# A polysketch attention and SwiGLU kernel on one core: the first batch cut into blocks of 384, 320 and 384 tokens, half of the third block's units multiplied by parts, and the key sums regrouped

## The chip, the cores and the metric

The kernel runs on one core of a Trainium2 chip. The engines of that core work side by side, each in its own order: TensorE (PE, matrix products into PSUM; PEld is its weight load), VectorE (DVE), ScalarE (ACT), GpSimd (POOL) and SyncE (SP), whose queue issues most of the DMA transfers. They wait for each other with semaphores. The metric is the device time of one execution in microseconds; lower is better. Three executions of the kernel before took 278.57, 278.71 and 279.0 us, so the median is 278.71.

## The reference

Inputs are q, k and v of 4 batches, 4 heads, 1088 tokens and 32 values (float32), two sketches S1 and S2 of 8 x 32, and the weights w_gate and w_val (128 x 1536) and w_out (1536 x 128). The sketches and weights come in 64-bit floats.

```python
def phi(x):                                   # 32 values -> 64 features
    a = np.einsum('rd,bhsd->bhsr', S1, x)
    b = np.einsum('rd,bhsd->bhsr', S2, x)
    return np.einsum('bhsi,bhsj->bhsij', a, b).reshape(*x.shape[:-1], r * r)
q_p, k_p = (phi(q), phi(k))
kv = np.einsum('bhsf,bhsd->bhfd', k_p, v)     # key values
z = np.sum(k_p, axis=2)                       # key sums
num = np.einsum('bhsf,bhfd->bhsd', q_p, kv)
den = np.einsum('bhsf,bhf->bhs', q_p, z)[..., None] + 1e-06
x = (num / den) as (4352 tokens, 4 heads * 32 = 128)
g, val = x @ w_gate, x @ w_val
out = (g * (1 / (1 + np.exp(-g))) * val) @ w_out
```

The attention has no softmax: a batch's keys are folded into one 64 x 32 matrix and one vector of 64 sums per head, and the queries are multiplied with these. Behind it stands a SwiGLU layer over all 4352 tokens with 1536 hidden values, by far the larger part of the work.

## The kernel before

**The layer.** Hidden values are cut into 12 chunks of 128. A *unit* (i, j) is chunk j of token block i: it multiplies the block's x with chunk j of w_gate and of w_val, applies SiLU on ScalarE and the product on VectorE, and leaves a tile of hidden values. A *down product* multiplies that tile with chunk j of w_out and adds it up over the 12 chunks in one PSUM bank; when a block's twelve are done, VectorE transposes the sum (`store`) and SP's queue sends it out.

Two kinds of units exist. A plain one (`unit`, matmuls at L1034) multiplies in float32, which the trace shows as two matmul records per product. A unit *by parts* (`start_unit`, L997, and `finish_unit`, L1010 and L1011) replaces each product by three in the single-pass format fp32r: x and the weights are first cut into a high part, a low part and a difference. `start_unit` multiplies the differences, ScalarE scales that PSUM pair in place (L1000), and `finish_unit` adds the two other products; ScalarE's SiLU (L1013) and VectorE's product (L1018) follow. The weights are cut by `cut_weights` (four steps for each quarter of a weight: high part on ScalarE, remainder on VectorE or GpSimd, low part on ScalarE, difference on VectorE or GpSimd, all L871), the tokens by `cut_tokens` (L881, L884, L889).

**The blocks.** The first batch's 1088 tokens are cut into three blocks, of 384, 384 and 320 tokens. Its attention is computed block by block, so that the layer can begin early, and all 36 units of these blocks are plain. The other three batches make seven blocks, six of 480 tokens and one of 384, called the *line*: their 84 units are by parts. In the line, unit y + 1 is started ahead of finishing unit y.

**PSUM.** Eight banks: g0, g1, g2 and acc (banks 0 to 3), and the pairs a (4, 5) and b (6, 7). Plain units take single banks in turn; from unit 17 of the list `seq` on only g0, g1 and g2 are in turn, and acc gathers the first block's down products. `pair` gives a line unit the least recently used of three pairs (g0 with g1, a, b).

**The order.** It is written out by hand; every engine keeps the order in which the program issues its instructions. The attention of batches 1 to 3 is the generator `attentions`, advanced some steps at a time by `parts_of` between units, and by `group` at fixed places in the line. For each batch it turns keys and queries (VectorE transposes, which also issue the next loads on SP's queue), multiplies the key sketches (L354), forms the key features on VectorE (L377, four operations over chunks 0 to 2, 3 to 4, 5 to 6 and 7 to 8, into the tile phk), adds the features of the nine chunks up on GpSimd (`feature_sums`, L547, five additions into zs), multiplies the key values (L388) and the sums (L717), folds them on VectorE (L601 to L608, the result is needed by the query sketches), spreads the key values by six DMAs on SP's queue (`spread_out`), multiplies the query sketches (L342), forms the query features (`query_step`: a denominator, then three rounds of features and transposes), and multiplies the numerators (L780). A place where the generator says `yield` is a place where units come between.

In before, the list `seq` holds 30 plain units behind the six that stand with the first batch's attention. From unit 17 on each is followed by one down product and one step of the second batch's attention, and by steps of the weight cutting. Then come the remaining down products in threes, with the second batch's numerators among them; behind these ("first") the third batch's key features and its five sums, the cutting of the line's first tokens, the first `start_unit`, the last two down products and the line:

```python
        phk = apool.tile([P, NC, H, R, R], FP32, tag="phk", name="phk")
        yield from features(phk, kab)
        zs, sums = feature_sums(phk)
        for f in sums:
            f()
        yield from turn_keys(3)
        yield from turn_queries(2)
        for b in (2, 3):
            yield "pe"
```

In the line, `parts_of` advances the generator by one step after each of the first twenty units, and `group` goes on to the next "pe" ahead of units 4, 6, 20, 22 and 40. What follows the first "pe" is the third batch's key values, key sketches of the fourth, and sums' products.

## Time and profile before

| | us |
|---|---|
| median of three executions | 278.71 |
| the profiled execution | 278.89 |
| its span (first to last instruction) | 277.2 |
| around the span | 1.69 |
| first plain unit's matmul (L1034) | 15.29 |
| first down product (L1082) | 49.01 |
| second batch: key sums on GpSimd (L547) | 63.20 to 68.89 |
| second batch: key values (L388), sums' products (L717), query products (L342) | 67.92, 68.95, 72.31 |
| second batch: numerators (L780) | 86.82 |
| first matmul of the line (L997) | 91.42 |
| third batch: key features (L377) | 91.17 to 93.93 |
| third batch: key sums on GpSimd | 93.49 to 99.34 |
| third batch: key values, sums' products, query products | 98.71, 101.06, 104.93 |

Times within the span are counted from its start. A row of a timeline gives the start, the duration, the engine, the line of the kernel, the operation with what it writes and reads, the shape and how many of them; in brackets stand the idle time of the engine ahead of it and what ended that. Durations overlap a little within an engine, as one operation's tail runs beside the next one's start, so a step is read from start to start. Matmul ends are modelled. In the chain of waits, times are moved by about 0.1 us against the timeline. The granted clock was 1.0 throughout.

### The profile page before, as it was taken

What the parts mean: (1) busy time and instruction counts of PE and PEld (TensorE: products, weight loads), DVE (VectorE), ACT (ScalarE), POOL (GpSimd) and SP (SyncE); (2) the same over time, 40 slices, a digit from 0 to 9 for tenths busy, and PEclk for the clock granted to TensorE, in tenths of its full rate; (3) what the DMA queues carried; (4) which work ended last, traced back from release to release, by engine and by line L of the source; (5) the groups of instructions that cost most, each with busy time, mean ns of one, the idle gap of its engine ahead of it and who ended that gap; (6) DMA issues with size and microseconds to landing.
All of it is one profiled execution on the core that took longest, in us unless ns stands there. A gap on an engine that the chain in (4) does not pass through costs nothing.

```text
span 277.2 us, 5670 instructions
## 1 busy us (share of the span) xinstructions
PE 271.4 (98%) x2169; PEld 198.3 (72%) x2169; DVE 203.7 (74%) x355; ACT 184.5 (67%) x330; POOL 98.9 (36%) x110
## 2 busy tenths in 40 slices
PE   8899999999999999999999999999999999999995
PEld 7645565666766787777577777867887888788994
DVE  3997987977688873887545766967877995987431
ACT  3468665565421586667479898769879878886860
POOL 3313422179820440060034353435425553542000
PEclk9999999999999999999999999999999999999999
DMA  6573195221151123000200020000100200010011
GB/s 192 168 220 79 54 277 185 74 89 57 39 114 28 26 85 94 2 1 0 38 13 4 0 39 0 0 2 10 27 0 2 36 0 1 9 29 0 10 29 28
DMA packets 26139, 14.30 MB, mean 52 GB/s; under 512 B 19840, under 2 KB 24192, under 8 KB 26112
## 3 DMA queue, kind: packets, MB, share of 16 engines
q1 hardware_dynamic: 25456, 13.84, 19.4%
q8 instruction: 17, 0.28, 0.4%
q10 hardware_dynamic: 656, 0.10, 0.2%
q14 instruction: 10, 0.08, 0.1%
HBM read 11.41 MB, written 2.23 MB: 49 GB/s over the span
## 4 chain that ended last, share of the span: by engine, by line
PE 94%; DVE 2%; DMA 2%; ACT 1%; issue 0%; SPq 0%
PE PS L1082 22%; PE PS L1034 16%; PE PS L1010 13%; PE PS L997 13%; PE PS L1011 13%; PE PS L1074 2%; PE PS L1077 2%; PE PS L1076 2%; PE PS L354 2%; PE PS L780 2%; PE PS L342 2%; PE PS L388 2%; DMA kld<-in_k_dram 2%; PE PS L1110 1%; PE PS L497 1%; PE PS L445 1%
## 5 line engine op out<-in xcount | busy, mean ns | idle before, releaser
L1000 ACT ACTIVATE PS<-PS 128x960 f32<-128x960 f32 (+1 forms) x84 | 78.5, 935 | 32.0 <-PE PS L997 31.2
L1018 DVE SCALAR_TENSOR_TENSOR hbuf<-PS,sg 128x480 f32<-128x480 f32 (+1 forms) x84 | 53.7, 640 | 43.6 <-ACT sg L1013 40.8
L1013 ACT ACTIVATE sg<-PS 128x480 f32<-128x480 f32 (+1 forms) x84 | 46.7, 556 | 2.0 <-PE PS L1011 1.2
L997 PE MATMUL PS<-xd,gphq 128*128 128x480 f32 (+1 forms) x84 | 47.3, 564 | 0.0
L1082 PE MATMUL PS<-hbuf,wo 128*128 128x480 f32 (+3 forms) x118 | 45.9, 492 | 0.0
L1010 PE MATMUL PS<-x,graw 128*128 128x480 f32 (+1 forms) x84 | 32.1, 382 | 0.0
L1011 PE MATMUL PS<-x,wb 128*128 128x480 f32 (+1 forms) x84 | 31.6, 376 | 0.0
L997 PE MATMUL PS<-xd,wd 128*128 128x480 f32 (+1 forms) x84 | 31.4, 374 | 0.0
L1010 PE MATMUL PS<-x,w 128*128 128x480 f32 (+1 forms) x84 | 31.4, 374 | 0.0
L1011 PE MATMUL PS<-x,graw 128*128 128x480 f32 (+1 forms) x84 | 31.3, 373 | 0.0
L1034 PE MATMUL PS<-xT,wg 128*128 128x384 f32 (+1 forms) x72 | 28.7, 480 | 0.0
L1034 PE MATMUL PS<-xT,wv 128*128 128x384 f32 (+1 forms) x72 | 28.0, 470 | 0.2 <-DVE wv L286 0.2
L1082 PEld LDWEIGHTS PS<-hbuf,wo 128*128 128x128 f32 x118 | 22.1, 189 | 7.4 <-issue 0.9
L1038 ACT ACTIVATE sg<-PS 128x384 f32<-128x384 f32 (+1 forms) x30 | 13.8, 465 | 18.8 <-PE PS L1034 17.2
L997 PEld LDWEIGHTS PS<-xd,gphq 128*128 128x128 f32 x84 | 15.8, 188 | 10.0 <-ACT PS L1000 6.4
L997 PEld LDWEIGHTS PS<-xd,wd 128*128 128x128 f32 x84 | 15.8, 189 | 9.9 <-issue 6.7
L884 POOL TENSOR_TENSOR x<-xT,x 128x480 fp32r<-128x480 f32 (+1 forms) x6 | 7.2, 1195 | 37.6 <-ACT x L881 37.6
L1034 PEld LDWEIGHTS PS<-xT,wv 128*128 128x128 f32 x72 | 13.4, 190 | 8.9 <-DVE hbuf L1049 0.9
L1034 PEld LDWEIGHTS PS<-xT,wg 128*128 128x128 f32 x72 | 12.9, 189 | 9.3 <-issue 1.2
L1010 PEld LDWEIGHTS PS<-x,graw 128*128 128x128 f32 x84 | 15.7, 187 | 3.5 <-ACT PS L1000 0.8
L1082 PE MATMUL PS<-hbuf,scaled 128*128 128x480 f32 x36 | 17.4, 565 | 0.0
L1010 PEld LDWEIGHTS PS<-x,w 128*128 128x128 f32 x84 | 15.8, 188 | 2.2
(184 smaller groups left out, 494.5 us busy)
## 6 DMA issues: line engine op xcount, KB each, us to landing
kld<-in_k_dram SPq DMA_DIRECT2D x4, 544.0 KB, 4.4
vld<-in_v_dram SPq DMA_DIRECT2D x12, 144.0 KB, 4.7
qld<-in_q_dram SPq DMA_DIRECT2D x3, 544.0 KB, 4.2
raw<-in_moe_w_out_dram SPq DMA_DIRECT2D x4, 384.0 KB, 4.0
raw<-in_moe_w_gate_dram SPq DMA_DIRECT2D x3, 384.0 KB, 3.6
raw<-in_moe_w_val_dram SPq DMA_DIRECT2D x3, 384.0 KB, 3.7
out_dram<-o SPq DMA_DIRECT2D x16, 60.0 KB, 2.0
vld<-in_v_dram SPq DMA_DIRECT2D x4, 112.0 KB, 4.3
```

Source lines behind the costliest of these rows:

```text
L342: nc.tensor.matmul(ps[32 * a : 32 * a + 32, 96 * (c - c0) : 96 * (c - c0) + 96], qT[:, 4 * c + a, :], s123[:, a : a + H, :, :].rearrange(" ...
L354: nc.tensor.matmul(ps[32 * a : 32 * a + 64, 64 * (c - c0) : 64 * (c - c0) + 64], kT[:, c, a : a + 2, :].rearrange("p a t -> p (a t)"), s12 ...
L884: engine.tensor_tensor(out=x0[:, 0:n], in0=x, in1=whole(x1[:, 0:n]), op=ALU.subtract)
L997: nc.tensor.matmul(ps[:, k], w_parts[id(w), j // 3][2][:, j % 3, :], xd, start=True, stop=True)
L1000: nc.scalar.activation(ps, ps, AF.Copy, scale=-1.0 / WHOLE)
L1010: nc.tensor.matmul(ps[:, k], w1, x1, start=False, stop=False, skip_group_check=True)
L1011: nc.tensor.matmul(ps[:, k], wb, x0, start=False, stop=True, skip_group_check=True)
L1013: nc.scalar.activation(sg, ps[:, 0], AF.Silu, scale=WHOLE)
L1018: nc.vector.scalar_tensor_tensor(out=hj[:, 0:n], in0=ps[:, 1], scalar=WHOLE, in1=sg, op0=ALU.mult, op1=ALU.mult)
L1034: nc.tensor.matmul(o[:, 0:n], w[:, j, :], xT[:, t0 : t0 + n], start=True, stop=True)
L1038: nc.scalar.activation(sg[:, 0:n], g[:, 0:n], AF.Silu)
L1082: nc.tensor.matmul(acc[i][:, 0:n], w, hidden[i, j][:, 0:n], **sides)
```

## The change

It has these parts:

- The first batch's blocks are 384, 320 and 384 tokens (`plan`).
- The third block's units 6 to 11 are no longer plain but by parts. `seq` has 24 units. Behind it stand thirteen more down products (twenty with the seven inside `seq`), taken in the order first block, then the second block's chunks 3 to 11 and 0 to 2; the second batch's attention steps and the cutting of the weights stand among them. Then the six units by parts, each with one down product, and behind them the numerators and ten more down products, with the line's first `start_unit` ahead of the last two.
- The weights are cut quarter by quarter, the third and fourth quarters first, for which the third block's tokens are cut too; for the first two quarters of w_gate the remainder and difference move from VectorE to GpSimd. The remainders of all of them are written into `room`.
- `feature_sums` adds chunks 0 and 1 to 2 and 3, then 4 and 5, then 6 and 7, in two rows of zs and not four. For the second batch each addition is issued as soon as its features are, so among the feature operations; the key sketches are multiplied ahead of the query transposes; PSUM for this attention comes from `pair`, not from a and b.
- In the second batch's group the key sketches of the third stand ahead of the sums' products. The output store of the first block, and its DMAs, stand ahead of the fold and the spread DMAs.
- Nothing advances the generator between "first" and the line. The third batch's key features thus stand behind the line's units 0 (one operation), 1 (two) and 2 (one); the five sums, the first key transpose, then, in the group ahead of unit 4, the second key transpose and the query transposes follow.

```diff
-    plan = [(HX + 2 - s) // 3 for s in range(3)]
+    plan = [6, 5, 6]
...
-        s = apool.tile([P, 4, H * F], FP32, tag="zs", name="zs")
+        s = apool.tile([P, 4, H * F], FP32, tag="zs", name="zs")[:, 0:2, :]
...
-            lambda: add(s[:, 0:2, :], rows[:, 0:2, :], rows[:, 4:6, :]),
-            lambda: add(s[:, 2:4, :], rows[:, 2:4, :], rows[:, 6:8, :]),
-            lambda: add(s[:, 0:2, :], s[:, 0:2, :], s[:, 2:4, :]),
+            lambda: add(s, rows[:, 0:2, :], rows[:, 2:4, :]),
+            lambda: add(s, s, rows[:, 4:6, :]),
+            lambda: add(s, s, rows[:, 6:8, :]),
             last,
...
         yield from turn_keys(1)
-        yield from turn_queries(1)
-        hold("a")
-        kp = wide("a")
+        kp = pair("keys")
...
+        yield from turn_queries(1)
         phk = apool.tile([P, NC, H, R, R], FP32, tag="phk", name="phk")
         for n, (i, c0, c1) in enumerate(((0, 0, 3), (0, 3, 5), (1, 5, 7), (1, 7, 9))):
...
             key_features(phk, (ka[:, H * c0 : H * c1, :], kb), c0, c1)
+            if n == 0:
+                zs, sums = feature_sums(phk)
+            else:
+                sums.pop(0)()
...
-        zs, sums = feature_sums(phk)
-        for f in sums:
-            f()
+        sums.pop(0)()
         yield from turn_keys(2)
-        kvz = wide("a")
+        kvz = pair("values")
         key_values(kvz[:, 0, 0:F], phk, 0, NC)
+        kab, copies = sketched(pair(), key_products, 2, "kab2")
+        run_copies(copies, 2)
         value_sums(kvz[:, 0, :], zs)
-        kab, kcopies = sketched(wide("b"), key_products, 2, "kab2")
         fold(kvz[:, 0, :])
...
-        yield
-        yield
-        numerators(1, spread, (wide("a"), wide("b")))
+        numerators(1, spread)
         yield "first"
...
-        first, second = (difference, low) if engine is nc.vector else (low, difference)
+        first, second = (difference, low) if soon else (low, difference)
...
-    seq += [(i, j) for j0 in (6, 9) for i in range(3) for j in range(j0, j0 + 3)]
-    order = [(i, j) for i in range(3) for j in range(NCH)]
+    seq += [(i, j) for j0 in (6, 9) for i in (0, 1) for j in range(j0, j0 + 3)]
+    order = [(0, j) for j in range(NCH)] + [(1, j) for j in range(3, NCH)] + [(1, j) for j in range(3)]
+    cuts = {"x": cut_tokens(2, nc.vector, soon=True)}
+    for c in (2, 3, 0, 1):
+        cuts["g%d" % c] = cut_weights(wg, c, free(8 + c % 2), nc.vector if c > 1 else nc.gpsimd)
+        cuts["v%d" % c] = cut_weights(wv, c, free(6 + c % 2), nc.gpsimd)
...
+    steps_at = {
+        0: ("g2", "v2", "v3"), 1: ("g2",), 2: ("g2", "g3"), 3: ("g3", "v2"), 4: ("g3", "v3"), 5: ("g2",),
+        7: ("x",), 8: ("x", "v0"), 9: ("g3", "v1"), 10: ("g0",), 11: ("g1",),
+    }
+    ND = 13
+    for n in range(ND):
+        if n == ND - 2:
+            start_unit(2, 6)
+        next_down()
+        parts_of(n in (0, 1, 5, 8, 10, 12))
+        at(*steps_at.get(n, ()))
+        if n in (5, 6, 7):
+            catch_up()
...
-    todo.sort()
-    x_steps = None
-    while len(todo) > 2:
-        for _ in range(min(3, len(todo) - 2)):
-            down()
-        if len(todo) < 9:
-            take(gates[3], 2)
-        if begun[0] and not x_steps:
-            x_steps = cut_tokens(HEAD, nc.vector)
-            run(x_steps)
-        parts_of(1 + (begun[0] and len(todo) > 2))
-    while not begun[0]:
-        parts_of(1)
...
+    todo.sort(key=lambda x: (order + [x]).index(x))
+    for j in range(6, NCH):
+        if j + 1 < NCH:
+            start_unit(2, j + 1)
+        finish_unit(2, j)
+        next_down()
+        parts_of(j in (6, 8))
+        at(*steps_at.get(j, ()))
+    parts_of(1)
+    x_steps = cut_tokens(HEAD, nc.vector, soon=True)
     while todo:
-        down()
+        if len(todo) == 2:
+            start_unit(HEAD, 0)
+        next_down()
+        next(x_steps, None)
```

The loop of the line, its groups and its attention steps from unit 4 on are unchanged.

## The prediction

> **What bounds the kernel now.** First the page's busy times and its chain of waits, then the timelines of the stretch that changes (48 to 102 us).
>
> ```profile
> PE 271.4 (98%) x2169; PEld 198.3 (72%) x2169; DVE 203.7 (74%) x355; ACT 184.5 (67%) x330; POOL 98.9 (36%) x110
> ...
> PEclk9999999999999999999999999999999999999999
> ...
> PE 94%; DVE 2%; DMA 2%; ACT 1%; issue 0%; SPq 0%
> ```
>
> TensorE is busy 98% of the span at full granted clock, and 94% of the chain is its own work. So the time moves by two things alone: TensorE work removed, and new waits of TensorE. Two rows price a unit, the first from the chain, the rest from TensorE's timeline in the last block, which also has 384 tokens:
>
> ```profile
> 62.19 1.29 PE PS L1034 x4
> ```
> ```profile
> 251.92 0.34 PE L997 MATMUL PS<-xd,gphq 128*128 128x384 f32 x1
> ...
> 252.97 0.38 PE L1074 MATMUL PS<-hlate,dparts 128*128 128x480 f32 x1
> ```
>
> A plain unit of 384 tokens takes 1.29 us; one by parts, from its first matmul to what follows it, 252.97 - 251.92 = 1.05 us (six steps of 0.175).
>
> Now the start of the third-batch group, in before: VectorE, then GpSimd, then ScalarE, then the chain.
>
> ```profile
> 91.17 2.76 DVE L377 TENSOR_TENSOR phk<-kab 128x768 f32<-128x768 f32 x4
> 93.84 0.51 DVE L1124 STREAM_TRANSPOSE o<-PS 128x320 f32<-128x320 f32 x1
> 95.33 0.66 DVE L1018 SCALAR_TENSOR_TENSOR hbuf<-PS,sg 128x480 f32<-128x480 f32 x1 [0.98 <-ACT sg L1013]
> 95.91 0.83 DVE L327 STREAM_TRANSPOSE kT<-kld 128x640 f32<-128x640 f32 x1
> 96.68 0.66 DVE L1018 SCALAR_TENSOR_TENSOR hbuf<-PS,sg 128x480 f32<-128x480 f32 x1
> ```
> ```profile
> 93.49 2.83 POOL L547 TENSOR_TENSOR zs<-phk 128x512 f32<-128x512 f32 x2 [11.22 <-PE PS L1082]
> 96.40 2.12 POOL L547 TENSOR_TENSOR zs<-zs 128x512 f32<-128x512 f32 x2
> 98.60 0.74 POOL L547 TENSOR_TENSOR zs<-zs,phk 128x256 f32<-128x256 f32 x1
> ```
> ```profile
> 93.87 0.95 ACT L1000 ACTIVATE PS<-PS 128x960 f32<-128x960 f32 x1 [0.62 <-PE PS L997]
> ```
> ```profile
> 98.78 1.14 PE PS L388 x72
> 99.93 1.20 PE PS L354 x36
> 101.12 0.25 PE PS L717 x8
> ```
>
> The reader is to see that the key features of the third batch (L377, four operations) were done at 93.9, before the first unit of the first line block had reached VectorE (95.33), and the five sums on GpSimd ended at 98.60 + 0.74 = 99.34, 1.8 us before TensorE needed them at 101.12 (L717). That margin is what the change uses up.
>
> **The change part by part.**
>
> 1. Six units of the third block by parts: 6 x (1.29 - 1.05) = **-1.4 us** of TensorE work. The 36 down products, the key, value and query products stay as many and as wide; they only move.
>
> 2. Blocks of 384, 320, 384: the columns of the three blocks add up as before, so TensorE's sum is unchanged but for step 1. What can differ is its small waits in the front: TensorE waited 0.24 us at 18.80 for a weight half on VectorE, and the unit that begins at 32.85 took 1.32 us where its 320 tokens need 1.08. The second block's smaller query features and divide spare VectorE some 0.25 us ahead of the first; units of 384 in place of 320 at 31 to 34 spare the second. But the first weight units now run out 3 x 0.215 = 0.65 us sooner, so the third block's query transposes (done at 22.37, TensorE at 22.48) can be late by up to 0.3. Between -0.4 and +0.3; I take **-0.15**, as both old waits are on VectorE work that shrinks.
>
> 3. Second batch's group. The sums now start after the second feature operation, so they overlap the features; they took 63.20 to 68.89 = 5.7 us. GpSimd's last part of w_out ended at 61.28 + 1.01 = 62.3 and comes about 1 us sooner with the front, so they end about 67.0. TensorE begins its down products at 49.01 in before, now at 49.01 - 0.65 - 0.15 = 48.2, and has until the sums' products 12 downs of 0.645, one of 0.54, three units of 1.29 and three of 1.08, two key products of 1.20 and the key values of 1.14: 19.0, so it wants them at 67.2. Hidden, by 0.2 us. Between the sums' products and the query products stood a unit and a down product; now three down products of 0.54 = 1.6 us. VectorE's fold took 69.33 to 70.90 = 1.57, with one operation held for 1.00 us beside GpSimd's work (0.23 at 102.02 without). Cost 0 to 0.3, I take **+0.1**. The output store and its four DMAs now stand ahead of the six spread DMAs on SP's queue: at 0.6 us per issue they end about 2.4 us later, near 74, and the numerators ask for them after 83; nothing.
>
> 4. The six units beside the query step. The units use three PSUM pairs, so the fifth one's first matmuls wait until VectorE has multiplied out the second. On VectorE that stands behind the query step. From the end of the query products: 0.6 until the copies are there (74.00 to 74.45, and the signal), 1.94 for the denominator (76.65 to 78.59), two rounds of features 1.0 and transpose 1.0, and two products of 0.55: 7.7 us. TensorE's own work up to that first matmul, in downs (0.54), starts (0.35) and finishes (0.70) of units, is 2 x 0.54 + 0.35 + 2 x 0.54 + 0.35, then 0.70 + 0.54 + 0.35, the same again, and 0.70 + 0.54 = 7.3 us. So 0.4 us late with nothing beside it. But GpSimd is now busy there with four remainders of the weights (about 1.0 each), which in before ran earlier or on VectorE. What that does to VectorE, from the third batch's sums in before (GpSimd first):
>
> ```profile
> 117.15 1.29 POOL L547 TENSOR_TENSOR zs<-late 128x512 f32<-128x512 f32 x1 [15.96 <-DVE late L377]
> ```
> ```profile
> 115.70 1.28 DVE L377 TENSOR_TENSOR late<-kab 128x512 f32<-128x512 f32 x2
> ...
> 117.82 1.17 DVE L377 TENSOR_TENSOR late<-kab 128x512 f32<-128x512 f32 x1
> ```
>
> A feature operation beside a GpSimd sum took 1.17, alone 0.64; the wide one 1.99 at 173.75 against 0.95; the dot 0.73 or 1.21 against 0.42. All held once adds some 1.9. So 0.4 to 2.3; I take **+1.0**, as the four remainders cover about half of the chain.
>
> 5. The third batch's group, the step that decides. The features are no longer done before the line: they stand on VectorE behind the products of units 0, 1 and 2 of the line, one, two and one at a time, and the sums run on GpSimd after them, with no other step between. Count from A, the start of ScalarE's drain of unit 1 (93.87 in before). TensorE reaches the sums' products at A + 101.12 - 93.87 = A + 7.25 by its own work, which does not change. Unit 0's product is at A + 95.33 - 93.87 = A + 1.46 (it waits for ScalarE, as before). Then 0.58 (95.33 to 95.91), the wide feature 0.87 (113.57 to 114.44), unit 1's product 0.58, the second feature 0.64: chunks 0 to 3 are there at A + 4.13. The signal to GpSimd 0.15, then the five sums, 93.49 to 99.34 = 5.85: A + 10.15. The wait is about 2.9 us; with the second batch's 5.69 it is 2.7, with the plain operations (3 x 1.28 + 0.85 + 0.74 = 5.4) 2.5. Features three and four (A + 4.8 and A + 6.0) and the two key transposes (A + 8.1) all end before the sums do. If features and sums hold each other in full, 2 x 0.64 more: 4.2. I take **+2.8**. Queued behind the waiting product on TensorE are all units from 5 on, so the wait is paid in full; VectorE's fold behind it was already paced by it.
>
> The row above has the feature held and the sum at its usual 1.29. The Trainium skill (GPSIMD Engine Reference, Key points) says that GpSimd shares its SBUF interfaces with VectorE and contends with operations of two SBUF inputs, which these features have; it speaks against moving features beside sums, but gives no price. By the row the sums lose nothing and the total is as below; by the rule read against GpSimd the total would be 1.3 us longer.
>
> Sum: -1.4 - 0.15 + 0.1 + 1.0 + 2.8 = +2.3 us. From the profiled execution (278.89: span 277.2 and 1.69 around it) that is 281.2; it lies 0.18 above the median 278.71, so **281.0** for the median.
>
> **The rivals.**
>
> (a) Faster: the sums' wait does not appear, because the features reach GpSimd so early that its last sum ends before A + 7.25. For it: the page has GpSimd 36% busy. Against it: VectorE works in order, so no feature can pass unit 0's product (done at A + 2.04), and 5.4 us of sums from there end at A + 7.4 without a single feature counted. It decides when 2.5 us vanish from that chain. It gives 278.7 - 1.4 - 0.15 = 277.2.
>
> (b) The wait at the sums alone, steps 3 and 4 hidden: 278.7 - 1.55 + 2.7 = 279.9. For it: VectorE's bare chain is only 0.4 late, and GpSimd may run in VectorE's gaps.
>
> (c) Both contentions at their upper ends: 278.7 - 1.5 + 0.3 + 2.0 + 3.7 = 283.2. For it: the 1.99 us row; against it: the sums' rows hardly differ (1.28 to 1.58).
>
> (d) The parts do not pay: a weight load takes 0.19, longer than a 0.175 step. Against it: in the last block loads and matmuls overlap and the step is still 0.175. It would add 6 x 6 x 0.015 = 0.5: 281.5, inside the range.
>
> **How the numbers follow.** My forecast, with (d) inside it: 0.55. (b): 0.27, of which 0.04 lie within 0.2% (a little less than 0.6 us, about what a measurement of this kernel can tell from no change), where step 5 is at 2.5 and the front gives 0.4. (c): 0.13. (a): 0.05, of which 0.01 within 0.2%. Faster 0.04, same 0.05, slower 0.91. The range 279.5 to 282.5 leaves out (a), the lowest of (b) and most of (c).
>
> **What would show it.** Right: in the changed profile TensorE waits for GpSimd at the sums' products of the third batch for 2 to 4 us, in the stretch 90 to 105, with the line's first unit about 0.5 to 1.5 us earlier than now; TensorE's busy time over units 6 to 11 of the third block is 1.05 us each; VectorE's products of those units delay a first matmul by 0.4 to 2. Wrong: no gap ahead of the sums' products (rival a), or a gap in the front above 0.5 us, for example at a weight half, which I have priced at nothing.

## The result, and the profile after

Four executions of the changed kernel took 283.19 to 283.87 us, median 283.38; the kernel before took 278.83 beside it. The ratio is 1.0167 with a 95% interval of 1.0149 to 1.0184: slower by 4.55 us, where 2.3 was forecast. The direction was right and the size was not; the time lies above the forecast range of 279.5 to 282.5.

The page of the changed kernel (busy times, granted clock, chain of waits):

```profile
PE 270.7 (96%) x2181; PEld 200.0 (71%) x2181; DVE 206.9 (73%) x353; ACT 189.7 (67%) x337; POOL 105.9 (38%) x114
...
PEclk9999999999999999999999999999999999999999
...
PE 83%; DVE 7%; POOL 4%; issue 2%; DMA 2%; ACT 1%; SPq 0%; POOLq 0%; DVEq 0%; ACTq 0%
```

TensorE has 0.7 us less work than before, but it is busy only 96% of a longer span, and 17% of the chain is not its own, where it was 6% before. The list of TensorE's waits (line, releaser, us in total, times, longest) names what ended them:

```profile
PE PS L715 <- POOL zs L547: 2.3, 2, 1.4
PE PS L354 <- DVE kT L327: 2.0, 2, 1.0
PE PS L982 <- DVE hbuf L1002: 1.0, 2, 0.7
...
PE PS L388 <- DVE phk L377: 0.6, 1, 0.6
```

L715 are the sums' products, once in the second batch's group and once in the third's. L982 are starts of the six units by parts. Of L354 one wait (0.98) is in the third batch's group; the other is the first key product of all, which waits for the first load of keys and comes at any time from 5.9 to 6.8 us in the profiles of this study, whatever the kernel. (In the profiled execution of the changed kernel, 283.87 us long, it came at 6.76; before, at 6.27.)

So I count from that first product. TensorE's timelines give the length of five stretches: I to the first down product, II on to the second batch's sums' products, III on to its numerators, IV on to the line's first start, V on to the third batch's sums' products. Behind V the kernels of the table need the same time within 0.4 us.

| us | I | II | III | IV | V |
|---|---|---|---|---|---|
| before | 42.74 | 19.94 | 17.87 | 4.60 | 9.64 |
| changed | 42.25 | 20.13 | 17.29 | 6.47 | 13.32 |
| features ahead (e1) | 42.25 | 20.11 | 17.28 | 6.47 | 9.86 |
| short remainders (e3) | 42.34 | 20.12 | 16.02 | 6.46 | 13.31 |
| plain units (e4) | 42.26 | 20.11 | 17.22 | 6.47 | 13.30 |
| all mended (e7) | 42.28 | 19.61 | 16.48 | 6.47 | 9.86 |
| features in line (e8) | 42.74 | 20.03 | 17.88 | 4.59 | 13.05 |

In I to IV the two kernels do different work (units and down products have moved: IV holds eight down products of 384 tokens where it had six of 320), so a difference there is not yet a loss. In V it is: only two of the down products are wider, by 0.2 together. The sum of the five is 94.79 before and 99.46 after: 4.67, which is the whole difference of the medians. V alone has 3.7 of it; up to the line's first start (I to IV) the changed kernel is 1.0 later, 86.14 against 85.15.

**Stretch V.** The same three engines as in the forecast, in the changed kernel: VectorE, GpSimd, TensorE.

```profile
97.07 0.66 DVE L1002 SCALAR_TENSOR_TENSOR hbuf<-PS,sg 128x480 f32<-128x480 f32 x1 [1.37 <-ACT sg L997]
97.65 0.95 DVE L377 TENSOR_TENSOR phk<-kab 128x768 f32<-128x768 f32 x1
98.51 0.65 DVE L1002 SCALAR_TENSOR_TENSOR hbuf<-PS,sg 128x480 f32<-128x480 f32 x1
99.08 1.28 DVE L377 TENSOR_TENSOR phk<-kab 128x512 f32<-128x512 f32 x2
...
100.85 1.22 DVE L377 TENSOR_TENSOR phk<-kab 128x512 f32<-128x512 f32 x1
...
102.56 1.42 DVE L327 STREAM_TRANSPOSE kT<-kld 128x640 f32<-128x640 f32 x2
```
```profile
99.93 1.58 POOL L547 TENSOR_TENSOR zs<-phk 128x512 f32<-128x512 f32 x1 [15.18 <-DVE phk L377]
101.59 2.97 POOL L547 TENSOR_TENSOR zs<-zs,phk 128x512 f32<-128x512 f32 x2
104.64 0.72 POOL L547 TENSOR_TENSOR zs<-zs 128x256 f32<-128x256 f32 x1
105.44 0.72 POOL L547 TENSOR_TENSOR zs<-zs,phk 128x256 f32<-128x256 f32 x1
```
```profile
100.50 0.99 PE L388 MATMUL PS<-phk,vld 128*32 128x64 f32 x56
102.12 0.43 PE L388 MATMUL PS<-phk,vld 128*32 128x64 f32 x16 [0.64 <-DVE phk L377]
103.53 1.27 PE L354 MATMUL PS<-s,kT 128*64 128x64 f32 x36 [0.98 <-DVE kT L327]
106.22 0.32 PE L715 MATMUL PS<-zs,ones 128*32 128x64 f32 x8 [1.42 <-POOL zs L547]
```

The reader is to see three waits in a row where before there was none: for the last features, for the turned keys, for the sums. All three stand behind the line's first units on VectorE, as step 5 said. The drain of unit 1 (A) is at 95.61, so the sums' products come at A + 10.6 where they came at A + 7.2.

**Stretches II and III.** At the second batch's sums, GpSimd, then VectorE, then TensorE:

```profile
59.02 1.96 POOL L848 TENSOR_TENSOR room<-wv,w 128x384 f32<-128x384 f32 x2
61.94 1.01 POOL L286 TENSOR_TENSOR wo<-man,exp 128x384 f32<-128x384 f32 x1 [0.96 <-DVE man L277]
62.90 1.28 POOL L547 TENSOR_TENSOR zs<-phk 128x512 f32<-128x512 f32 x1
...
68.17 0.92 POOL L547 TENSOR_TENSOR zs<-zs,phk 128x256 f32<-128x256 f32 x1
```
```profile
60.33 1.06 DVE L271 SCALAR_TENSOR_TENSOR exp<-raw,exp 128x384 int32<-128x384 int32 x1
...
63.38 0.68 DVE L377 TENSOR_TENSOR phk<-kas,PS 128x512 f32<-128x512 f32 x1
...
75.97 1.66 DVE L377 TENSOR_TENSOR phq<-qab 128x768 f32<-128x768 f32 x1
...
78.63 0.52 DVE L1002 SCALAR_TENSOR_TENSOR hbuf<-PS,sg 128x384 f32<-128x384 f32 x1
79.07 1.20 DVE L377 TENSOR_TENSOR phq<-qab 128x768 f32<-128x768 f32 x1
```
```profile
69.14 0.32 PE L715 MATMUL PS<-zs,ones 128*32 128x64 f32 x8 [0.85 <-POOL zs L547]
...
77.20 0.33 PE L982 MATMUL PS<-xd,wd 128*128 128x384 f32 x1
77.36 0.34 PE L994 MATMUL PS<-x,graw 128*128 128x384 f32 x1
...
79.20 0.44 PE L982 MATMUL PS<-xd,wd 128*128 128x384 f32 x1 [0.26 <-DVE hbuf L1002]
79.48 0.34 PE L994 MATMUL PS<-x,graw 128*128 128x384 f32 x1
...
81.78 0.44 PE L982 MATMUL PS<-xd,wd 128*128 128x384 f32 x1 [0.73 <-DVE hbuf L1002]
82.06 0.34 PE L994 MATMUL PS<-x,graw 128*128 128x384 f32 x1
```

Beside GpSimd's operations, VectorE's operations with two inputs in SBUF take longer here: the w_out step L271 1.06 (0.55 at 56.95, with GpSimd idle), the query features 1.66 and 1.20 (0.95 alone). The same kind of operation with one input in PSUM is not touched: key features from kas and PS took 0.68 beside a sum. The two L982 rows that waited follow their own unit's first matmul (78.36 and 80.48) by 0.84 and 1.30 in place of 0.42: 0.42 + 0.88 = 1.3 lost. And the matmul behind each comes 0.28 after it, where it is 0.16 without a wait (77.20 to 77.36): a stop also costs some 0.11 of the overlap between matmuls. So the six units lost 1.5 in all.

### The profile page after: what moved, and what is told of

Same layout as the page of the kernel before. It is cut to its first block, busy times and chain, and to the rows that moved or that the text cites. A ratio compares the mean times of both kernels' runs of the same rounds, so it can differ in the third digit from the quotient of the medians.

```text
span 282.1 us, 5723 instructions
## 1 busy us (share of the span) xinstructions
PE 270.7 (96%) x2181; PEld 200.0 (71%) x2181; DVE 206.9 (73%) x353; ACT 189.7 (67%) x337; POOL 105.9 (38%) x114
## 3 DMA queue, kind: packets, MB, share of 16 engines
q1 hardware_dynamic: 25456, 13.84, 19.3%
## 4 chain that ended last, share of the span: by engine, by line
PE 83%; DVE 7%; POOL 4%; issue 2%; DMA 2%; ACT 1%; SPq 0%; POOLq 0%; DVEq 0%; ACTq 0%
PE PS L1070 19%; PE PS L994 13%; PE PS L982 13%; PE PS L995 12%; PE PS L1018 11%; POOL zs L547 4%; PE PS L1065 2%; PE PS L1062 2%; PE PS L1064 2%; PE PS L778 2%; PE PS L342 2%; DMA kld<-in_k_dram 2%; DVE hbuf L1002 1%; DVE phq L377 1%; PE PS L1098 1%
## 5 line engine op out<-in xcount | busy, mean ns | idle before, releaser
L985 ACT ACTIVATE PS<-PS 128x960 f32<-128x960 f32 (+1 forms) x90 | 83.3, 926 | 37.0 <-PE PS L982 36.0
L997 ACT ACTIVATE sg<-PS 128x480 f32<-128x480 f32 (+1 forms) x90 | 49.6, 551 | 2.6 <-ACT sg L997 1.3
L982 PE MATMUL PS<-xd,graw 128*128 128x480 f32 (+1 forms) x69 | 38.3, 556 | 0.0
L982 PE MATMUL PS<-xd,wd 128*128 128x480 f32 (+1 forms) x90 | 33.8, 376 | 1.0 <-DVE hbuf L1002 1.0
L982 PEld LDWEIGHTS PS<-xd,wd 128*128 128x128 f32 x90 | 17.0, 189 | 12.2 <-issue 6.0
L995 PE MATMUL PS<-x,graw 128*128 128x480 f32 (+1 forms) x69 | 25.5, 370 | 0.0
L1018 PE MATMUL PS<-xT,wg 128*128 128x384 f32 (+1 forms) x60 | 23.5, 474 | 0.1
L1018 PE MATMUL PS<-xT,wv 128*128 128x384 f32 (+1 forms) x60 | 23.2, 467 | 0.3 <-DVE wv L286 0.3
L1022 ACT ACTIVATE sg<-PS 128x384 f32<-128x384 f32 (+1 forms) x24 | 11.2, 468 | 13.2 <-PE PS L1018 12.4
L982 PEld LDWEIGHTS PS<-xd,graw 128*128 128x128 f32 x69 | 13.0, 188 | 7.7 <-ACT PS L985 4.0
L995 PEld LDWEIGHTS PS<-x,wb 128*128 128x128 f32 x90 | 16.9, 188 | 2.1
L994 PE MATMUL PS<-x,graw 128*128 128x480 f32 (+1 forms) x48 | 18.4, 383 | 0.0
L962 POOL TENSOR_TENSOR hlate<-hbuf,hlate 128x480 fp32r<-128x480 f32 x10 | 12.9, 1291 | 9.8 <-ACT hlate L961 7.7
```

The costliest lines, as they stand in the source:

```text
L962: add_to(before, y + 2, lambda: nc.gpsimd.tensor_tensor(out=h0, in0=h, in1=whole(h1), op=ALU.subtract))
L982: nc.tensor.matmul(ps[:, k], w_parts[id(w), j // 3][2][:, j % 3, :], xd, start=True, stop=True)
L985: nc.scalar.activation(ps, ps, AF.Copy, scale=-1.0 / WHOLE)
L994: nc.tensor.matmul(ps[:, k], w1, x1, start=False, stop=False, skip_group_check=True)
L995: nc.tensor.matmul(ps[:, k], wb, x0, start=False, stop=True, skip_group_check=True)
L997: nc.scalar.activation(sg, ps[:, 0], AF.Silu, scale=WHOLE)
```

## The experiments

Theory: step 5 is real but a little dearer than forecast, and the rest of the miss is small contentions at the second batch's sums and at the six units. The rival to each is that the engines are late there whatever the order.

**Step 5, undone and alone.** First the changed kernel with the features and sums ahead of the line again:

```diff
         next_down()
-        next(x_steps, None)
+        if next(x_steps, "done") == "done":
+            parts_of(ahead[0] != "sums")     # "sums" is a new yield behind the sums
```

> The changed kernel with one thing undone: the third batch's four key features and five sums are issued behind the cutting of the line's first tokens, ahead of the last down products, and no longer behind units 0 to 3 of the line. In the profile of the changed kernel TensorE waits in the line for key features (0.64 us), turned keys (0.98) and sums (1.42), together 3.0 us, and reaches the sums' products 10.6 us after ScalarE's drain of unit 1 where it was 7.2 before. Theory (step 5 of the prediction, undersized): all of this goes, and nothing later turns up: 283.4 - 3.2 = 280.2, between 279.9 and 280.6; the sums end some 4 us ahead of their products. The prediction's own 2.8 would give 280.6. Rival: the place is not the cause, VectorE or GpSimd are late there whatever the order (the query step ends later than before), and less than half comes back: 282 or more.

Measured: 279.78 us (12 executions), ratio 1.0024 (1.0008 to 1.0041); 3.6 less than the changed kernel and just under the range of the theory. V fell by 3.46, and no other stretch moved. On TensorE all three waits are gone, and the sums (GpSimd) end 4 us early:

```profile
100.40 1.21 PE L388 MATMUL PS<-phk,vld 128*32 128x64 f32 x72
101.54 1.27 PE L354 MATMUL PS<-s,kT 128*64 128x64 f32 x36
102.74 0.32 PE L716 MATMUL PS<-zs,ones 128*32 128x64 f32 x8
```
```profile
97.88 0.74 POOL L547 TENSOR_TENSOR zs<-zs,phk 128x256 f32<-128x256 f32 x1
```

Then the kernel before, with nothing but this step in it:

```diff
-        parts_of(1 + (begun[0] and len(todo) > 2))
+        parts_of(not begun[0])       # and the changed feature_sums
```

> The kernel before with one part of the change alone: the third batch's four key features and its sums (in the changed kernel's grouping) are no longer advanced ahead of the line, but one step behind each of its first units. Blocks, units, weight cuts and the second batch stay as they were. By the prediction's step 5 this costs 2.8: 281.6. Theory from the profile of the changed kernel, where the sums' products came 10.6 us behind the drain of unit 1 in place of 7.2: 3.2 to 3.6, so 282.0 to 282.4. Rival: the step is only dear together with the rest, since here the line's first tokens are cut and VectorE is free earlier: 280.8 or less.

Measured: 283.23 (282.47 to 286.55), ratio 1.0167 (1.0127 to 1.0208); the profiled execution took 282.62. The stretches are the clean reading: V is 3.41 longer, the others are unchanged, and the same three waits stand there (0.61, 0.98, 1.42). Undone or alone, the step is worth 3.4 to 3.5; the theory holds and the rival falls. Three of the six executions are 1.2 to 4 us longer still, which puts the median 0.8 above the theory's range. The record has their mean granted clock: 283.83 and 284.05 us at 0.994, 286.55 at 0.988, where the three others (282.47 to 282.62) have 0.998 or 0.999. The last section says what such a figure means.

**Does the wait cost its own length?** One addition is done twice:

```diff
+        sums[0]()
         for f in sums:
             f()
         yield from turn_keys(3)
```

> The changed kernel with the first of the third batch's five additions on GpSimd done twice, with the same result: the sums end some 1.5 us later, the wait ahead of their products grows from 1.42 to about 2.9. Theory of the prediction (every microsecond that the sums are late is paid once and in full, as all units stand behind them on TensorE): 283.4 + 1.5 = 284.9. Theory with the clock: in an earlier run a wait of 2.25 us was followed by 3.8 us at half the granted clock, which cost another 1.5; here the waits of 0.6, 1.0 and 2.9 lie within 6 us, so the granted clock drops behind them in most executions: 285.6 to 287.5, with a granted clock near 0.5 in some microseconds behind 108. Rival: the sums do not set the end of that stretch: 283.4 to 284.

Measured: 286.10 (286.01 to 286.44), 2.7 more than the changed kernel. V grew by 1.34 (13.32 to 14.66), as the sums' theory has it; the other 1.4 came behind it. TensorE, and then busy times by window (us; PE, PEld, DVE, ACT, POOL, the granted clock, DMA share, GB/s):

```profile
107.08 0.32 PE L716 MATMUL PS<-zs,ones 128*32 128x64 f32 x8 [2.75 <-POOL zs L547]
```
```profile
108.00:110.00 2.00, 2.00 (x8) 1.62 (x7) 0.91 (x4) 1.43 (x2) 0.20 (x1) 0.55 0.05 11
110.00:112.00 2.00, 2.00 (x6) 1.51 (x5) 0.38 (x2) 1.43 (x2) 0.00 (x0) 0.60 0.08 17
112.00:114.00 2.00, 2.00 (x74) 1.48 (x72) 0.53 (x1) 0.40 (x1) 0.00 (x0) 1.00 0.15 30
```

Behind the wait TensorE ran at 0.55 to 0.60 of its clock for some 4 us. The theory with the clock was right, to the size. All five executions have a mean granted clock of 0.994.

**Step 4, contention or order.** GpSimd's steps for the first two quarters of the weights are cut short:

```diff
+        m = 8 if c < 2 else P
-        engine.tensor_tensor(out=low, in0=src, in1=whole(w1), op=ALU.subtract)
+        engine.tensor_tensor(out=low[:, :, 0:m], in0=src[:, :, 0:m], in1=whole(w1)[:, :, 0:m], op=ALU.subtract)
...
+            if c < 2:
+                engine.memset(whole(wd), 0.0)
```

> The changed kernel with GpSimd's load beside the query step taken away: of the remainders of the first two quarters of w_gate and w_val only 8 of 128 columns are formed, and their differences are set to zero in place of being computed, so the line's products with these quarters are not the reference's. GpSimd is then free from about 75 us on, where it was busy to 84.7. TensorE lost 0.42 and 0.88 us there, ahead of the fourth and fifth of the six units' starts by parts. Theory (contention, the prediction's upper end): VectorE's query step runs at its lone durations and both waits go, 282.1, between 281.9 and 282.4. Rival 1 (order, the prediction's lower end): 0.4 stays, since VectorE's products stand behind the query step anyway: 282.5. Rival 2: contention with GpSimd is not the cause: 283.2 or more.

Measured: 282.36 (281.82 to 284.89), ratio 1.0133 (1.0093 to 1.0173). By the stretches III is shorter by 1.27, and neither start has a listed wait. VectorE in that run:

```profile
74.96 0.96 DVE L377 TENSOR_TENSOR phq<-qab 128x768 f32<-128x768 f32 x1
...
77.37 0.94 DVE L377 TENSOR_TENSOR phq<-qab 128x768 f32<-128x768 f32 x1
```

The features take 0.95 again. The step is contention, 1.3 of its 1.5 us. Of the order alone 0.25 is left: 0.14 at the fifth start (79.26 to 79.82, where 0.42 is normal) and 0.11 behind it.

**Step 1, plain units again.** 

```diff
-        if n == ND - 2:
-            start_unit(2, 6)
...
-        if j + 1 < NCH:
-            start_unit(2, j + 1)
-        finish_unit(2, j)
+        unit(2, j, apart=True)
```

> The changed kernel with the last six units of the third block multiplied plainly again, in the same places, each in one PSUM pair; the cutting of the weights and of the block's tokens stays, so the work of the other engines is nearly the same. By the prediction six units cost 6 x 0.24 = 1.4 us more, and the 1.0 for the waits ahead of the starts goes, as the plain units take 1.83 us each with their down product and come later: 283.8. With the waits at the 1.3 us that the profile shows, and some 0.1 of one left at the fifth: 283.5 to 283.6. Rival (parts do not pay, a weight load and changes between formats eat the gain): 282.3 or less.

Measured: 283.22 (283.02 to 283.86), 0.16 below the changed kernel, which is within both spreads. III is 17.22 against 17.29: the waits with what they cost, 1.5, are gone, no wait is left there, and 1.4 of plain work has come in their place. So the parts pay the forecast 1.4, and rival (d) falls; in the changed kernel the contention took back what they paid. The expectation of 283.5 to 283.6 had counted the waits at 1.3.

**Step 3, two tries.** First both remainders behind the sums:

```diff
-    steps_at = {20: ("v2",), 21: ("v3", "v2", "v3"), 22: ("g2",), 23: ("g3",)}
+    steps_at = {20: ("v2",), 21: ("v3",), 22: ("g2",), 23: ("g3",)}
...
-        0: ("g2", "v2", "v3"), 1: ("g2",), 2: ("g2", "g3"), 3: ("g3", "v2"), 4: ("g3", "v3"), 5: ("g2",),
+        0: ("g2", "v2", "v3"), 1: ("g2",), 2: ("g2", "g3"), 3: ("g3",), 4: ("g3",), 5: ("v2", "v2"), 6: ("v3",), ... 8: ("v3", "x", "v0"), ...
```

> The changed kernel with one thing moved: the two remainders of w_val's last two thirds that GpSimd forms ahead of the second batch's key sums (59.02 to 60.98 in its profile) are formed behind them, and their low parts and differences follow later. Theory: these two held up VectorE's step for w_out's last part (1.06 us in place of 0.55), so GpSimd's multiplication of that part and with it the sums came some 0.9 us late; TensorE's wait of 0.85 us at the second batch's sums goes: 282.6, between 282.4 and 282.9. Rival 1: the sums wait for the features themselves, and the order on GpSimd is no matter: 283.4. Rival 2: the GpSimd work that moves back by 2 us holds VectorE's query step for longer, and the 0.85 comes back at the six units: 283.2 to 283.8.

Measured: 286.46 (284.96 to 286.92), ratio 1.0243 (1.0211 to 1.0275): 3 us slower than the changed kernel, a miss for every theory, though of rival 2's kind. The wait at the sums did fall, from 0.85 to 0.33. But two low parts now stood on ScalarE ahead of the token cut (x, L867) and the copies of the query sketches (qab), waiting for GpSimd; counted from the first key product, VectorE's query step began 0.6 later (67.3 against 66.7) where TensorE was 0.5 ahead, its first operations were held by 0.8 (L743 1.11 where it took 0.46, L748 0.40 where it took 0.25), and one start waited 2.25 us. ScalarE and TensorE:

```profile
70.24 0.52 ACT L850 ACTIVATE wb<-room 128x384 fp32r<-128x384 f32 x1 [0.43 <-POOL room L848]
70.67 0.51 ACT L867 ACTIVATE x<-xT 128x384 fp32r<-128x384 f32 x1
71.20 1.14 ACT L590 COPY qab<-PS 128x480 f32<-128x480 f32 x2
```
```profile
80.11 0.41 PE L982 MATMUL PS<-xd,wd 128*128 128x384 f32 x1 [2.25 <-DVE hbuf L1002]
```

Here too the clock fell behind the wait (windows, columns as above). The two executions whose clock did not fall (284.96 and 285.14) are 1.7 over the changed kernel, so some 1.4 of the 3 us is the clock's:

```profile
79.00:80.00 1.00, 0.00 (x0) 0.00 (x0) 1.00 (x3) 0.00 (x0) 1.00 (x2) 1.00 0.02 8
...
81.00:82.00 1.00, 1.00 (x5) 0.80 (x3) 0.97 (x3) 1.00 (x3) 1.00 (x2) 0.50 0.00 0
82.00:83.00 1.00, 1.00 (x4) 0.58 (x3) 1.00 (x4) 0.57 (x2) 1.00 (x2) 0.50 0.00 0
```

Then only the last quarter's remainder, with its low part behind those copies:

```diff
-    steps_at = {20: ("v2",), 21: ("v3", "v2", "v3"), ...
+    steps_at = {20: ("v2",), 21: ("v3", "v2"), ...
-        3: ("g3", "v2"), 4: ("g3", "v3"), ... 9: ("g3", "v1"), 10: ("g0",), 11: ("g1",),
+        3: ("g3", "v2"), 4: ("g3",), ... 9: ("g3", "v1", "v3"), 10: ("g0", "v3"), 11: ("g1",),
```

> The changed kernel with one remainder (of w_val's last quarter) formed on GpSimd behind the second batch's sums and not ahead of them; its low part follows on ScalarE only behind the copies of the query sketches, and its difference on GpSimd behind the products caught up there. When both remainders were moved, the wait at the sums fell from 0.85 to 0.33, but two low parts on ScalarE then stood ahead of the token cut and the query copies and made the query step 0.5 us later against TensorE. Theory: here ScalarE is not held, the step for w_out on VectorE takes 0.55 again in place of 1.06, the wait at the sums falls to 0.3 or 0.4, and step 4 stays as it was: 282.9, between 282.6 and 283.1. Rival 1: the query step meets TensorE 0.5 us sooner than in the changed kernel, since TensorE has gained it and VectorE not, and the gain is given back ahead of the six units' starts: 283.3 or more. Rival 2: the sums start no sooner with only one remainder away: 283.4.

Measured: 283.24 (282.97 to 284.48), ratio 1.0158 (1.0136 to 1.0181), which cannot be told from the changed kernel. By the trace the wait at the sums fell to 0.34 and II by 0.52 (to 19.61), and III gave 0.14 back: a net 0.38. So 0.5 of the 0.85 comes from a single remainder of 1 us; 0.33 or more stayed in every arrangement that was tried.

**Step 2, the block sizes alone,** in the kernel before:

```diff
-    plan = [(HX + 2 - s) // 3 for s in range(3)]
+    plan = [6, 5, 6]
```

> The kernel before with one part of the change alone: the first batch's blocks of 384, 320 and 384 tokens. TensorE's columns add up as before. By the prediction 0.15 us are saved: 278.65 where the kernel before has 278.8. Theory from the profile of the changed kernel: from its first key product to its first down product 42.25 us pass, before 42.74; the shorter units make 0.65 of it, so 0.16 was lost to small waits for VectorE (a weight half, the third block's turned queries), and that stays: 278.95, between 278.7 and 279.3. Rival: in this order of units the block of 320 tokens comes at a worse place than in the changed kernel, and VectorE's or GpSimd's products come late: 279.5 or more.

Measured: 280.79 (280.55 to 282.29), ratio 1.0080 (1.0054 to 1.0106): slower by 2.0, as its rival had it. Stretch I is 42.25, as in the changed kernel: 0.49 shorter, where shorter units alone make 0.65. The loss comes later: the second block's down products, now narrower, bring TensorE to the numerators before VectorE has turned the query features, the first of which took 1.79 beside GpSimd:

```profile
87.90 1.57 PE L780 MATMUL PS<-phT,spread 32*32 32x288 f32 x64 [1.18 <-DVE phT L762]
```

Another 0.32 is waited for the second batch's sums. The wait at the numerators does not exist in the changed kernel, where the query step comes earlier; what the two runs have in common is stretch I.

**All mended.** Features ahead (e1), one remainder behind (e6), and the first two quarters of both weights cut only when the query step's features are done:

```diff
-        6: ("v0", "v1", "g0"), 7: ("g1", "v0", "v1"), 8: ("g0", "g1", "v0"), 9: ("v1", "g0"), 10: ("g1",),
+        9: ("v0", "g0", "v0", "g0"), 10: ("v0",), 11: ("g0", "v0", "g0", "v1", "g1", "v1", "g1"),
     }
+    late_cuts = ("v1", "g1", "v1", "g1")      # behind the line's first token cut
```

> The changed kernel with three things rearranged: the third batch's features and sums ahead of the line again (which gave 279.8 alone), the one remainder behind the second batch's sums, and the first two quarters of both weights cut later, so that GpSimd's eight steps for them (some 10.6 us) begin when the query step's last features are done and end just ahead of the third batch's sums. Theory: three contentions made the loss, so with all of them gone the time is the kernel before less the 1.4 of the units by parts and some 0.3 of the front, plus what is left of the second batch's wait (0.3) and of the six units' (0.1 to 0.5): 278.0, between 277.6 and 278.5. Rival 1: the later weight cuts meet the numerators and the line's first tokens on VectorE and ScalarE, or push the third batch's sums on GpSimd beyond their products (7.2 us behind the drain of unit 1): 279.5 or more. Rival 2: only one of the two smaller mends works: 278.6 to 279.3.

Measured: 278.54 (12 executions, 278.31 to 280.38), ratio 0.9990 (0.9973 to 1.0006). The large loss is gone, 4.8 us from the changed kernel, but the theory's 278.0 was missed, and the interval holds no change against the kernel before; by the stretches it is 0.1 shorter. Two of the new waits on TensorE behind the first down product are left:

```profile
67.83 0.32 PE L716 MATMUL PS<-zs,ones 128*32 128x64 f32 x8 [0.34 <-POOL zs L547]
...
79.51 0.44 PE L983 MATMUL PS<-xd,wd 128*128 128x384 f32 x1 [0.30 <-DVE hbuf L1003]
```

Two further tries at these waits, in the same kernel, moved the three catch-up products (hbuf<-hbuf,room on GpSimd, 3.4 us in all) into GpSimd's idle time. The first put one into each of three units and had the last step of w_out's last part one unit earlier; the second issued all three at once and had the third block's queries turned earlier:

```diff
-        if n in (5, 6, 7):
-            catch_up()
...
+        if z in (18, 19, 20):        # the second try: if z == 18, three times
+            catch_up()
```

> The rearranged kernel (278.5) with two more moves on GpSimd and VectorE: the three products that catch up the second block's first hidden tiles (3.4 us on GpSimd, so far beside the second batch's token cut and denominator) are formed some 20 us earlier, where GpSimd idles for 7.3 us, and the last step of w_out's last part comes one unit earlier, ahead of the key features. In the rearranged kernel TensorE still waits 0.34 at the second batch's sums and loses some 0.46 at the six units' starts. Theory: VectorE operations with two SBUF inputs are held by GpSimd (token cut 1.20 against 0.66, the product with the denominator 0.78 against 0.46), those with one input in PSUM are not; with the catch-ups gone from there the query step is 0.9 us earlier and the starts do not wait; the sums' wait falls to 0.1: 277.8, between 277.5 and 278.2, faster than the kernel before. Rival: the earlier products hold VectorE's conversion of w_out's parts, and with them the features or a unit's bank: 278.5 or more.

> The rearranged kernel (278.5) with two moves: the three products that catch up the second block's first hidden tiles are all issued on GpSimd behind unit 18 of the list, in the middle of its idle stretch (in the trial before, the third of them came at 59.0 us and held VectorE's step for w_out to 1.22 and so the second batch's sums); and the third block's queries are turned on VectorE ahead of the third quarter's weight conversion, where TensorE waits 0.16 us for them. Theory: the sums' wait stays at 0.34, the query step is free of GpSimd, so 0.3 to 0.45 come back at the six units' starts, and 0.15 in the front: 278.0, between 277.7 and 278.3, faster than the kernel before. Rival: both stretches only push the next wait forward (ScalarE's copies of the query sketches, a weight quarter): 278.4 or more.

Measured: 278.80, ratio 1.0000 (0.9990 to 1.0010), and 278.91, ratio 1.0002 (0.9991 to 1.0012). Both missed. In the first, the third product came only at 59.0 and the sums' wait grew to 0.58; in the second, the queries' wait of 0.16 gave way to one of 0.31 at 27.58 for a weight part on GpSimd. The units' start still waits 0.26 in both: III is 16.44 against 16.48. VectorE's query step there ran at its lone durations but for one operation, the TENSOR_SCALAR at L749 (L748 in e3), which took 0.53 where e3 has 0.25, beside the difference of the last quarter on GpSimd (73.67 in e9, 73.46 in e11). Those 0.28 are just what the start came later than in e3 (0.83 or 0.84 and not 0.56 behind its unit's first matmul). It fits; it was not tested.

## Why the prediction was wrong in size

| step | forecast | measured | from |
|---|---|---|---|
| 1 units by parts | -1.4 | -1.4 | e4 against the changed kernel, with its 1.5 of waits |
| 2 block sizes, front | -0.15 | +0.16 | stretch I shorter by 0.49, the shorter units are 0.65 |
| 3 second batch's group | +0.1 | +0.85 | wait at 69.14; 0.5 of it shown by e6 |
| 4 six units | +1.0 | +1.5 | e3, III by 1.27, and 0.25 left there |
| 5 third batch's group | +2.8 | +3.4 | e1 3.46, e8 3.41 |
| sum | +2.3 | +4.5 | 4.55 by the medians |

Step 5 was the right mechanism in the right place, and a term of it was mis-sized: the five sums. All up to their start was met: features of chunks 0 to 3 were forecast at A + 4.13 and were there at A + 4.15. The sums then took 6.23 (99.93 to 106.16) and not 5.85. That is 0.4 of the 0.6 that was missing; 0.1 is that I took 2.8 where my sum with 5.85 said 2.9, and the last 0.1 lies in small steps between the engines. TensorE does not take these 3.4 us in one wait, as I had it, but in three (3.04 us as listed, and some 0.1 of overlap lost at each stop): I had looked at features and turned keys only as to whether they end before the sums, not at the key values and key sketches that wait for them. This does not make the total longer, since the sums end last; it is why the wait at their products is 1.42 and not the 2 to 4 that I gave as a sign.

The row that I trusted has a held feature beside a sum of 1.29. There the sum had started first (117.15, the feature at 117.82). In the changed kernel two sums began while a feature was running, and there the sum is held: the first (99.93, beside a feature until 100.36) took 1.58 and the second (101.59, beside one until 102.07) 1.61, where the second batch's first took 1.28. One of these was in the forecast's 5.85 already (1.58 at 93.49, beside a feature until 93.93), as I had not seen; the other is 0.3 of the 0.4. The rule that I set against the row (the Trainium skill, GPSIMD Engine Reference, Key points: GpSimd shares its SBUF interfaces with VectorE and contends with operations of two SBUF inputs) would have made the total 1.3 longer; by the sums' length, 0.4 of this 1.3 came. That the rule speaks of two SBUF inputs agrees with the 0.68 of L377 from kas and PS, which stays free. It names one more kind, operations in a 2-port mode; the runs do not show modes, but e9's L749, with a single input, was longer too (0.53 against 0.25).

Step 3 failed as argued. I called the sums hidden by 0.2 us, with two margins: GpSimd's last w_out part 1 us sooner with the front, and the sums 5.7 long. TensorE wanted them 19.3 behind the first down product (forecast 19.0), but they ended 20.1 behind it (forecast 18.8): the w_out part was late because VectorE's step for it was held beside two remainders, which I had only counted where they run beside the query step, and the sums took 6.2. Step 2 failed on a wait that I had named (the turned queries, 0.16) and a gap of 0.18 at 30.2 that I had not; of the two old waits that I expected to shrink, the weight half stayed (0.27 at 19.15). Step 1 came out as forecast.

Step 4 came out 0.5 over what I took, inside its bounds of 0.4 to 2.3, with its parts otherwise divided: of the order alone 0.25 remains, not 0.4, and the contention is nearly all of it.

So 0.6 of the miss of 2.2 lies in step 5, and 1.6 in steps 2 to 4, ahead of the line. The line's first unit shows this: I expected it 0.5 to 1.5 earlier, and it came 1.0 later.

Of the rivals, (a) and (b) fall with the waits seen. (c) named nearly the right time, 283.2, but by other terms: steps 4 and 5 stayed below its upper ends, and the rest came from steps 2 and 3. That its total is so near is luck. What the range had wrong is that I treated the steps as if their errors would cancel; every one but the first was dearer than forecast. What steps 3, 4 and 5 cost above their forecasts has in the main one cause, VectorE and GpSimd side by side in SBUF. For steps 3 and 4 the experiments show it (e6, e3); for the 0.4 of step 5 it is read from the rows.

## What to carry to other kernels

Where a change moves work on GpSimd, list every VectorE operation that works from SBUF alone and now runs beside it, not only those of the stage in question, and price each at its lone time and a good part of the GpSimd operation beside it. In the rows read here as much as 1.04 us was added, beside GpSimd operations of 1.0 to 1.6: that doubled a feature operation of 0.95 (1.99 in the forecast's row) and made four times of a small one (L608, 1.00 against 0.23). These errors add up and do not cancel. Work that many units wait for on one engine should stand ahead of the first unit, in the idle time that is already there: the same nine operations cost nothing there and 3.4 us four units later. A step that is moved out of the way takes its successors on the other engines along: a low part on ScalarE that waits for GpSimd holds whatever stands behind it.

## What was not expected of the hardware

**Waits below 3 us can cost the clock, and not in every execution.** In e2 a listed wait of 2.25 us was followed by 0.50 of the granted clock for some 3.4 us; in e10 waits of 0.6, 1.0 and 2.75 within 6 us by 0.55 to 0.60 for 4 us, which made 1.4 us of its time. In the profiled execution of the changed kernel, with 0.6, 1.0 and 1.4 us, the clock stayed at 1.00. But in e2's, behind the same three waits, it fell a second time:

```profile
108.00:110.00 2.00, 2.00 (x9) 1.70 (x6) 0.99 (x4) 0.92 (x2) 0.83 (x1) 0.52 0.72 259
110.00:112.00 2.00, 2.00 (x7) 1.68 (x6) 0.66 (x1) 1.03 (x3) 0.00 (x0) 0.63 0.09 21
```

Each of the three falls takes as much from the clock as 3.4 us at one half. An execution's mean granted clock therefore tells the falls: e10's profiled one, with one, has 0.994, e2's, with two, 0.988. By this reading the changed kernel had none in its four executions and e4 none in five; one of e6's five had one, two of e3's six, and three of e8's six, one of them two falls. All have the same three waits, and the executions with a fall are each kernel's longest, by at least 1 us. What decides whether it falls, no run shows. The Trainium skill (TensorE: Matmul & The Clock Gate, Part 1) has the throttle fall after at least one idle window of about 3.4 us; here less than that was enough, three times, with no stretch of 3 us in which TensorE did nothing.

**The start is noise.** The first key product came at 5.94 to 6.77 us in thirteen profiles, as the first load landed; that alone moves a whole execution by 0.8 us, more than some of the steps above.
